# fe in row layout by a transposing transfer, out stores issued from ScalarE, and the last chunk's u in one step

## The chip, the cores and the metric

One core of one Trainium2 chip. The time is device time in microseconds (us) of one launch; the number to predict is the median over runs. TensorE is called PE, VectorE DVE, ScalarE ACT, GpSimd POOL, SyncE SP.

## What is computed

The forward pass and all gradients of a small speech encoder with a joint network (bfloat16, B=2, T=16000, D=V=256, U=8):

```python
h  = gelu(conv3(x, w1))[:, ::2]            # [2, 8000, 256]
f  = gelu(conv3(h, w2))[:, ::2]            # [2, 4000, 256]
fe = f @ w_f ;  ge = g @ w_g               # [2, 4000, 256], [2, 8, 256]
j  = tanh(fe[:, :, None, :] + ge[:, None, :, :])
out = j @ w_o                              # [2, 4000, 8, 256]
out, vjp = jax.vjp(forward, x, w1, w2, g, w_f, w_g, w_o)
return (out, *vjp(grad_out))
```

## The kernel before

The 8000 positions of `f` are cut into 17 chunks: one of 2x128, fifteen of 4x128 (`CW` = 512) and a last one of 1x64 (`LAST` = 16). Three stages work on different chunks at once: `stage_j(k)` (tanh, `out`, and what flows back to fe), `stage_a(k+1)` (convolutions, gelu, fe) and `stage_de(k-1)` (all other gradients). PE does the matmuls; ACT and DVE share the element work; SP issues nearly all transfers.

The order of instructions on each engine isn't the order of the source. `Flow.op` records every operation with a place (`F.now` or `at`, in positions: 512 of them are one full chunk), a modelled cost and what it depends on. `Flow.issue` then fills the engines one instruction at a time by modelled start time, then by place. Numbers such as 0.55 of `dt`, `late`, `land` (the time assumed between a transfer's end and its use) or `lag` (an extra wait in the model only) thus only move an operation in its engine's queue. Each engine works through its queue in that fixed order, and an instruction whose input isn't there holds up all behind it.

What the change touches, for a chunk g:

- `FE` (L593 on) holds fe with the 256 channels on partitions, as [128, 2, 512]; two evacuations write it. `stage_j` reads it for tanh into `JT` (L670), with `ge` as the bias.
- From chunk 2 on (`NTR` = 2), `fe_rows` also makes `FER`, fe with positions on partitions: 8 PE transposes into one PSUM tile (L616) and one copy (L324 or L329). For each pair of u, DVE then adds `GEB` to `FER` (L694) and ACT takes tanh in place (L699); the result `JR` is the weight operand of the matmuls into `GWO`, the gradient of w_o, which stays in PSUM for the whole run. `JR` and `OUT` each have 3 buffers. Chunks 0 and 1 make `JR` by PE transposes of `JT` (L688).
- A chunk's `stage_j` goes in 4 pairs of u. Each pair loads `GO` (grad_out), makes `GOT` from it by a transposing transfer, and stores `OUT`. All of these are issued by SP (L339 the transposing transfers, L341 the others). In the last chunk the same instructions have 64 positions instead of 128 or 512.
- The gradients of a chunk need rows too: `HR`, `GNR` and `GHR` are transposing transfers from SP, by `tile_rows`.
- The last gradients end with `last_w1`, `last_gx_stores` and small stores. At the start, ACT issues the loads of w1, w_f and w_g, and POOL that of w_o.

Of the kernel before, what the change touches and what calls it, by code (L numbers as in the profile page):

```python
# [35 lines left out]
class Flow:  # L36
# [70 lines left out]
    def issue(self):  # L107
# [14 lines left out]
        while left:  # L122
# [40 lines left out]
            if o.xfer:  # L163
                kind, work, land = o.xfer
                if e == "SP":
                    work, gap = self.ring(dma_kind, kind, work, dma_free)
                    begin = max(dma_free + gap, s + 1300.0)
                    dma_free, dma_kind = begin + work, kind
                    T[e] = max(T[e], dma_free - self.BACKLOG[kind])
                    o.done = dma_free + land  # L170
                else:
                    o.done = T[e] + work + land
            else:
                o.done = T[e] + self.TAIL[e]
# [14 lines left out]
def c_pe(ns):  # L189
    return sum(max(n / 2.4 + 2.5, 25.0) for n in ns)  # L190
# [20 lines left out]
def kernel(  # L211
# [254 lines left out]
    def conv_gelu(g_, jobs, rd, h_buf, pre, ho, gname, gcls, gshape, gsave, news):  # L466
# [39 lines left out]
        late = F.now + CW * (0.8 if g_ == 1 else 0.25)  # L506
# [34 lines left out]
    def stage_a(g_, t0, dt):  # L541
# [25 lines left out]
        F.now = t0 + 0.05 * dt  # L567
# [3 lines left out]
        F.now = t0 + 0.12 * dt  # L571
# [3 lines left out]
        F.now = t0 + 0.3 * dt  # L575
# [15 lines left out]
        F.now = t0 + 0.48 * dt  # L591
        FE = S["FE"] = buf("fe", [P, KT, CW], BF16, "FE")
        for mt in range(KT):  # L593
            ps = psum()

            def mms(e, mt=mt, ps=ps):
                for kt in range(KT):
                    mm(ps[:, :c.W], WF[:, kt, mt * P:(mt + 1) * P], HT[:, oF:oF + nb, kt, :n_], kt == 0, kt == KT - 1)
            op("PE", c_pe([c.W] * KT), mms, r=ftk + [WF], w=[ps], new=[ps] + ([FE] if mt == 0 else []))
            evac(lambda mt=mt: FE[:, mt, :c.W], lambda ps=ps: ps[:, :c.W], c.W, r=[ps], w=[(FE, mt)])  # L600
        F.now = t0 + 0.55 * dt
        if g_ >= NTR:
            fe_rows(g_)
        F.now = t0 + 0.75 * dt
        tile_rows(g_, "HR", "hr", HT, 3 * nb + 1, shape=[P, 3 * NB + 1, D], land=4500.0)

    def fe_rows(g_):
        c, S = chunks[g_], st[g_]
        nb, n_, FE = c.nb, c.np, S["FE"]
        FER = S["FER"] = buf("fer", [P, NB, D], BF16, "FER")  # L610
        ps = psum(BF16)

        def trs(e, ps=ps):
            for a in range(nb):
                for kt in range(KT):
                    nc.tensor.transpose(out=ps[:n_, (a * KT + kt) * P:(a * KT + kt + 1) * P],  # L616
                                        in_=FE[:, kt, a * n_:(a + 1) * n_], identity=ident[:])
        op("PE", c_pe([P] * (nb * KT)), trs, r=[FE, ident], w=[ps], new=[ps, FER])
        evac(lambda: FER[:n_, 0:nb].rearrange("p a d -> p (a d)"), lambda ps=ps: ps[:n_, 0:nb * D], nb * D,
             r=[ps], w=[FER], f=0.5)  # L620

    n_gwo = sum(c.nb for c in chunks) * U * KT
# [29 lines left out]
    def stage_j(g_, t0, dt):  # L654
# [4 lines left out]
        def cut(ap, lo, hi):  # L659
            return ap.rearrange("p (a n) -> p a n", a=nb)[:, :, lo:hi] if c.mid else ap  # L660

        def pair(up):
# [4 lines left out]
            for j in range(2):  # L667
                for mt in range(KT):
                    for k_, (lo, hi, b) in enumerate(parts_of(c)):
                        op("ACT", c_act((hi - lo) * nb, ptr=True), lambda e, j=j, mt=mt, lo=lo, hi=hi, b=b: nc.scalar.activation(  # L670
                            out=cut(JT[:, j, mt, :W], lo, hi), in_=cut(S["FE"][:, mt, :W], lo, hi), func=ACT.Tanh,
                            bias=GE[:, b, mt, 2 * up + j:2 * up + j + 1], scale=1.0),
                           r=[(S["FE"], mt), (GE, b)], w=[(JT, (j, mt, k_))],
                           new=[JT] if j == 0 and mt == 0 and k_ == 0 else [], at=tu - q * (1.0 - (2 * j + mt) / 4))
            npart = len(parts_of(c))
            for h in range(max(nb // 2, 1)):
                na = min(nb, 2)
                JR = buf("jr", [P, 2, 2, D], BF16, "JR")
                th = tu + q * (h / 2 - 0.5)
# [30 lines left out]
                gwo_ops.append(op("PE", c_pe([V] * (4 * na)), gwo, r=[JR, GO], w=[], at=tu + q * (h / 2 + 0.3)))  # L710
            OUT = buf("out", [P, NB, 2, V], BF16, "OUT_SB")
            for step in range(4):
# [12 lines left out]
                if d2 == 0:  # L725
                    JSQ = buf("jsq", [P, KT, CW], BF16, "JSQ")

                    def jsq(e, j=j, JSQ=JSQ):
# [5 lines left out]
                       r=[(JT, (j, mt, k_)) for mt in range(KT) for k_ in range(npart)], w=[JSQ], new=[JSQ], at=F.now - q / 4)  # L734
# [22 lines left out]
                if step < nb:  # L757
# [8 lines left out]
                    op("PE", c_pe([V] * 4), out_mm, r=[JT, WO, (OUT, "b")], w=[ps], new=[ps] + ([OUT] if a == 0 else []))  # L766
# [4 lines left out]
            dma("SP", lambda dst_=dst_: dst_, lambda OUT=OUT: OUT[:n_, 0:nb].rearrange("p a u v -> p a (u v)"), r=[OUT], w=[],  # L771
                bytes_=W * 1024)
# [5 lines left out]

    def pe_rows(g_, name, cls, SRC, lo, nblk, m):
        R = buf(cls, [P, 2 * NB + (cls == "ghr"), D], BF16, name)  # L780
# [8 lines left out]
        op("PE", c_pe([P] * (nblk * KT)), trs, r=[SRC, ident], w=[ps], new=[ps, R])  # L789
# [3 lines left out]
    def grad_rows(g_, name, cls, SRC, nblk, m):  # L793
        if chunks[g_].last:
            return pe_rows(g_, name, cls, SRC, 1, nblk, m)
# [42 lines left out]
    def stage_de(g_, t0, dt):  # L838
# [15 lines left out]
        F.now = t0 + dt * 0.05  # L854
# [68 lines left out]
        load_xr(g_, t0 - 300.0 if c.last else t0 + dt * 0.3, [got_op[0, UP - 1]] if c.first else ())  # L923
# [139 lines left out]
    def gwg_out():  # L1063
# [10 lines left out]
    CONVS = 4  # L1074
    GEBX = 1.2
# [5 lines left out]
       r=[(warm, 0)], w=[(warm, 1)])  # L1081
# [17 lines left out]
    wload("ACT", WG, 0, lambda: WG[:], lambda: w_g.rearrange("(kt p) n -> p kt n", p=P), BIG, 7000.0)  # L1099
# [5 lines left out]
    wload("POOL", WO, 0, lambda: WO[:], lambda: w_o.rearrange("(kt p) n -> p kt n", p=P), BIG + 2, 9000.0)  # L1105
# [51 lines left out]
    for k in range(NG + 1):  # L1157
        c = chunks[min(k, LAST)]
        t0, Wk = float(c.q0 if k < NG else NQ), float(c.W) if k < NG else 300.0
        if k < NG:  # L1160
            if k in (NTR, CB, CB + 1):
                load_geb(c, lambda up, t0=t0, Wk=Wk, k=k: t0 + Wk * (up / UP - (GEBX if k == NTR else 0.5)))
            for up in range(UP):
                load_go(k, up, t0 + Wk * (up // 2 * 2 / UP - 0.6), [got_op[0, up - 2]] if k == 0 and up > 1 else ())
                load_got(k, up, t0 + Wk * (up / UP - 0.6))
        if 0 < k < LAST:
            load_xc(k + 1, t0 - Wk * 0.3)
        if k < NG:
            stage_j(k, t0, Wk)
# [49 lines left out]
```

## Time and profile before

| | |
|---|---|
| median of 3 runs | 782.3 us (781.51 to 782.38) |
| profiled execution, its own time | 781.06 us |
| its span | 779.0 us, 2.06 us less than its own time |
| granted PE clock | 0.999 |
| busy: PE, DVE, ACT, POOL | 767.7, 718.2, 710.5, 84.0 us |
| transfers | 183.82 MB, 236 GB/s in the mean |
| out stores of 512 KB, issue to landing | 60 of them, 5.5 us median |

Times are microseconds from the span's start, and ns where said. A row of the grouped view has line, engine, operation, output and inputs, tile shapes, count; then busy time and the mean ns of one. In the timeline each row is a start, a length, an engine and an operation with its count; an engine name with q (ACTq, SPq) is the issuing of a transfer or a wait in that engine's queue. Matmuls overlap, so what one costs is read from one row's start to the next row's start, not from its length.

### The profile page before, as it was taken

The numbers are of one execution on the slowest core, as the hardware profiler recorded it, in microseconds if no ns is written. First come the engines' busy times: TensorE is split into PE (matmuls) and PEld (weight loads), VectorE is DVE, ScalarE is ACT, GpSimd is POOL, SyncE is SP. The second block draws the span as 40 slices with busy tenths as digits, with TensorE's granted clock in tenths as the row PEclk, the third lists the DMA queues.
The fourth block names the chain that finished last, engine by engine and source line by source line (L and its number), as shares of the span: only waits on it lengthen the run. The fifth ranks groups of instructions, "written<-read, shape, count | busy, mean of one in ns | idle before, by whom it ended". The sixth has DMA issues, their size and how long they took to land.

```text
span 779.0 us, 15414 instructions
## 1 busy us (share of the span) xinstructions
PE 767.7 (99%) x5641; PEld 533.0 (68%) x5641; DVE 718.2 (92%) x1511; ACT 710.5 (91%) x1145; POOL 84.0 (11%) x223
## 2 busy tenths in 40 slices
PE   8999999999999999999999999999999999999997
PEld 6765767576676766767577675766767667677765
DVE  4989999998999999999999999989999899999874
ACT  5989999999999999999999999899999999999752
POOL 2001010101102010020110202001020010201000
PEclk9999999999999999999999999999999999999999
DMA  9999999999999999999999999999999999989783
GB/s 182 228 250 230 230 232 265 250 228 273 205 252 241 240 293 223 280 236 238 257 252 283 204 249 252 236 283 212 272 238 223 254 223 291 191 225 244 187 177 109
DMA packets 393624, 183.82 MB, mean 236 GB/s; under 512 B 318145, under 2 KB 386668, under 8 KB 391628
## 3 DMA queue, kind: packets, MB, share of 16 engines
q1 hardware_dynamic: 391226, 181.64, 102.5%
q10 hardware_dynamic: 2178, 1.05, 0.5%
q8 instruction: 44, 0.72, 0.4%
q0 software_dynamic: 144, 0.15, 0.2%
q14 instruction: 32, 0.26, 0.1%
HBM read 52.99 MB, written 50.35 MB: 133 GB/s over the span
## 4 chain that ended last, share of the span: by engine, by line
PE 89%; ACT 6%; DVE 3%; DMA 2%; issue 1%; ACTq 0%
PE ps L315 74%; PE GWO L315 14%; ACT JT L670 2%; DMA WG<-in_w_g_dram 1%; PE psb L616 1%; ACT JSQ L730 1%; ACT HT L499 1%; ACT g_sq L497 1%; DMA W<-in_w_dram 0%; DVE NGZ L739 0%; ACT JR L699 0%; ACT OUT_SB L324 0%; DVE g_s L501 0%; DVE ZS L754 0%; ACT g_s L509 0%
## 5 line engine op out<-in xcount | busy, mean ns | idle before, releaser
L670 ACT ACTIVATE JT<-FE,GE 128x512 bf16<-128x512 bf16 (+4 forms) x288 | 178.9, 683 | 0.0
L739 DVE SCALAR_TENSOR_TENSOR NGZ<-JSQ,ps 128x512 f32<-128x512 bf16 (+3 forms) x252 | 150.8, 607 | 2.1 <-PE ps L315 1.9
L315 PE MATMUL ps<-WO,JT 128*128 128x256 bf16 (+1 forms) x1008 | 150.5, 273 | 0.3 <-DVE NGZ L739 0.2
L315 PE MATMUL ps<-GOT,WOT 128*128 128x512 bf16 (+2 forms) x544 | 149.9, 362 | 0.3 <-DVE g_s L501 0.3
L730 ACT ACTIVATE JSQ<-JT 128x1024 bf16<-128x1024 bf16 (+2 forms) x129 | 131.0, 1015 | 11.1 <-DVE NGZ L739 8.3
L315 PEld LDWEIGHTS <-JT 128*128 128x128 bf16 (+1 forms) x1008 | 98.3, 98 | 58.3 <-issue 0.4
L324 ACT CAST OUT_SB<-ps 128x512 bf16<-128x512 f32 (+1 forms) x205 | 121.7, 605 | 14.8 <-PE ps L315 14.3
L699 ACT ACTIVATE JR<-JR 128x1024 bf16<-128x1024 bf16 (+1 forms) x116 | 123.5, 1066 | 9.6 <-DVE JR L694 9.6
L315 PE MATMUL GWO<-GO_R,JR 128*128 128x256 bf16 (+1 forms) x1008 | 130.8, 273 | 0.6 <-DVE JR L329 0.6
L754 DVE TENSOR_TENSOR ZS<-ZS,NGZ 128x1024 f32<-128x1024 f32 (+2 forms) x102 | 115.3, 1130 | 0.7
L315 PEld LDWEIGHTS <-JR 128*128 128x128 bf16 (+1 forms) x1008 | 98.2, 98 | 15.8 <-DVE JR L329 0.9
L315 PEld LDWEIGHTS <-W 128*128 128x128 bf16 x636 | 60.0, 98 | 59.8 <-issue 0.7
L315 PE MATMUL ps<-W1T,GH 128*128 128x256 bf16 (+2 forms) x506 | 94.6, 325 | 1.3 <-ACT FE L324 1.2
L315 PE MATMUL ps<-XC,W 128*128 128x512 bf16 (+2 forms) x432 | 86.5, 351 | 0.1
L315 PE MATMUL ps<-GHR,XR 128*128 128x256 bf16 (+1 forms) x736 | 83.3, 273 | 0.0
L315 PEld LDWEIGHTS <-XR 128*128 128x128 bf16 (+1 forms) x756 | 73.7, 98 | 8.6
L694 DVE TENSOR_TENSOR JR<-FER,GEB 128x1024 bf16<-128x1024 bf16 (+1 forms) x116 | 78.0, 673 | 0.0
L315 PEld LDWEIGHTS <-WOT 128*128 128x128 bf16 x544 | 51.0, 98 | 29.6 <-issue 1.9
L819 DVE TENSOR_TENSOR ACC<-ACC,ps 128x512 f32<-128x512 f32 x87 | 57.4, 679 | 14.4 <-PE ps L315 14.3
L315 PEld LDWEIGHTS <-GH 128*128 128x128 bf16 (+1 forms) x506 | 49.4, 98 | 26.3 <-issue 1.9
L326 ACT ACTIVATE GX_SB<-ps 128x512 bf16<-128x512 f32 (+1 forms) x89 | 52.0, 608 | 13.8 <-PE ps L315 13.5
L497 ACT ACTIVATE g_sq<-ps 128x512 bf16<-128x512 f32 (+2 forms) x102 | 57.6, 565 | 2.8 <-PE ps L315 2.8
(131 smaller groups left out, 984.2 us busy)
## 6 DMA issues: line engine op xcount, KB each, us to landing
GO_R<-in_grad_out_dram SPq DMA_DIRECT2D x60, 512.0 KB, 5.2
out_dram<-OUT_SB SPq DMA_DIRECT2D x60, 512.0 KB, 5.5
XR<-in_x_dram SPq DMA_DIRECT2D x15, 1088.0 KB, 8.6
out_dram<-GX_SB SPq DMA_DIRECT2D x30, 512.0 KB, 3.3
GOT<-GO_R SPq DMA_TRANSPOSE x68, 5.3
GO_R<-in_grad_out_dram SPq DMA_DIRECT2D x4, 256.0 KB, 4.1
out_dram<-OUT_SB SPq DMA_DIRECT2D x4, 256.0 KB, 2.6
out_dram<-STAGE SPq DMA_DIRECT2D x6, 128.0 KB, 1.8
```

Of the source, the lines that this page charges most:

```text
L315: nc.tensor.matmul(ps_ap, lhsT=lhsT, rhs=rhs, start=start, stop=stop)
L324: nc.scalar.copy(out=dst(), in_=src())
L326: nc.scalar.activation(out=dst(), in_=src(), func=ACT.Copy, scale=scale)
L497: op("ACT", c_act(W, True), lambda e, mt=mt, ps=ps: nc.scalar.activation(out=sq[:, 0:nb, mt, :n_], in_=blk(ps, c), func=ACT.Square, scale= ...
L499: op("ACT", c_act(W, True), lambda e, mt=mt, ps=ps: nc.scalar.activation(out=h_buf[:, ho:ho + nb, mt, :n_], in_=blk(ps, c), func=ACT.Gelu_ ...
L670: op("ACT", c_act((hi - lo) * nb, ptr=True), lambda e, j=j, mt=mt, lo=lo, hi=hi, b=b: nc.scalar.activation(out=cut(JT[:, j, mt, :W], lo, h ...
L694: op("DVE", c_dve(na * 2 * D, 0.5), lambda e, h=h, na=na, JR=JR: nc.vector.tensor_tensor(out=JR[:n_, 0:na], in0=S["FER"][:n_, 2 * h:2 * h ...
L699: op("ACT", c_act(na * 2 * D), lambda e, na=na, JR=JR: nc.scalar.activation(out=JR[:n_, 0:na], in_=JR[:n_, 0:na], func=ACT.Tanh), r=[JR], ...
L730: nc.scalar.activation(out=JSQ[:, :, :W], in_=JT[:, j, :, :W], func=ACT.Square)
L739: nc.vector.scalar_tensor_tensor(out=cut(Z[:, d2, :W], lo, hi), in0=cut(JSQ[:, d2, :W], lo, hi), scalar=1.0, in1=cut(ps[:, :W], lo, hi), o ...
L754: nc.vector.tensor_tensor(out=o_, in0=i0, in1=i1, op=ALU.add)
L819: op("DVE", c_dve(512), lambda e: nc.vector.tensor_tensor(out=acc_ap().rearrange("p k d -> p (k d)"), in0=acc_ap().rearrange("p k d -> p ( ...
```

## The change

- `FE` becomes [128, 4, 2, 128], the layout that `tile_rows` takes. For chunks 2 to 15 `fe_rows` is one transposing transfer of 256 KB on SP, instead of 8 PE transposes and a copy. The last chunk has no `FER` any more.
- The `OUT` stores of chunks 0 to 15 are issued from ACT's queue, placed in the model 2.5 us after their data is there (`lag`).
- `stage_j_last` replaces `stage_j` for chunk 16: its 64 positions of 8 u are one tile of 512 columns. Two loads, one transposing transfer, 8 transposes of `JT` for `JR`, 4 matmuls of 512 columns (before 32 of 64), 8 out and 8 `GWO` matmuls with 128 positions (before 16 and 16 with 64), two stores.
- Places and model terms: longer landing times, a least PE cost of 45 ns instead of 25, the `JR` work 0.41 of a pair's time later, the `GWO` matmuls 0.04 earlier, `HR` from 0.75 to 0.43 of a chunk, the next chunk's `XC` load earlier, and others. w_o is loaded from ACT's queue instead of POOL's, and the first activation comes after those loads.

```diff
-    return sum(max(n / 2.4 + 2.5, 25.0) for n in ns)
+    return sum(max(n / 2.4 + 2.5, 45.0) for n in ns)
...
-        F.now = t0 + 0.48 * dt
-        FE = S["FE"] = buf("fe", [P, KT, CW], BF16, "FE")
+        F.now = t0 + 0.46 * dt
+        FE = S["FE"] = buf("fe", [P, NB, KT, P], BF16, "FE")
...
-        F.now = t0 + 0.55 * dt
-        if g_ >= NTR:
+        F.now = t0 + 0.63 * dt
+        if NTR <= g_ < LAST:
             fe_rows(g_)
-        F.now = t0 + 0.75 * dt
+        F.now = t0 + 0.43 * dt
         tile_rows(g_, "HR", "hr", HT, 3 * nb + 1, shape=[P, 3 * NB + 1, D], land=4500.0)

     def fe_rows(g_):
         c, S = chunks[g_], st[g_]
         nb, n_, FE = c.nb, c.np, S["FE"]
+        if not c.last:
+            return tile_rows(g_, "FER", "fer", FE, nb, shape=[P, NB, D], at=F.now - 400.0, land=7000.0)
...
-                th = tu + q * (h / 2 - 0.5)
+                th = tu + q * (h / 2 - 0.09)
...
-                gwo_ops.append(op("PE", ..., gwo, ..., at=tu + q * (h / 2 + 0.3)))
+                gwo_ops.append(op("PE", ..., gwo, ..., at=tu + q * (h / 2 + 0.26) + DEFER.get((g_, up), 0.0)))
...
-            dma("SP", lambda dst_=dst_: dst_, lambda OUT=OUT: ..., r=[OUT], w=[],
-                bytes_=W * 1024)
+            dma("SP" if c.last else "ACT", lambda dst_=dst_: dst_, lambda OUT=OUT: ..., r=[OUT], w=[],
+                bytes_=W * 1024, lag=0.0 if c.last else 2500.0)
...
+    def stage_j_last(t0):
...
+                op("ACT", ..., out=JT[:, 0, mt, u * n_:(u + 1) * n_], in_=S["FE"][:, 0, mt, :n_], func=ACT.Tanh, ...
+                   at=t0 - 64.0)
...
+        op("PE", c_pe([P] * (UP * KT)), trs, r=[JT, ident], w=[tr], new=[tr, JR])
+        evac(lambda: JR[:].rearrange("p a d -> p (a d)"), lambda: tr[:], UP * D, r=[tr], w=[JR], f=0.5)
...
+    DEFER = {(LAST - 1, 3): 100.0, (LAST - 1, 2): 130.0}
...
-    wload("POOL", WO, 0, lambda: WO[:], ..., BIG + 2, 9000.0)
+    wload("ACT", WO, 0, lambda: WO[:], ..., BIG, 7000.0)
...
-                load_go(k, up, t0 + Wk * (up // 2 * 2 / UP - 0.6), ...)
-                load_got(k, up, t0 + Wk * (up / UP - 0.6))
+                load_go(k, up, t0 + Wk * (up // 2 * 2 / UP - 0.66), ...)
+                load_got(k, up, t0 + Wk * (up / UP - 0.51))
...
-            load_xc(k + 1, t0 - Wk * 0.3)
+            load_xc(k + 1, t0 - Wk * 0.58)
...
-            stage_j(k, t0, Wk)
+            stage_j(k, t0, Wk) if k < LAST else stage_j_last(t0)
```

136 lines of the change are left out of this document (112 added, 24 removed).

## The prediction

> **What bounds the kernel now.** I read the page first: the shares of the engines, the DMA slices, and the chain that ended last.
>
> ```profile
> span 779.0 us, 15414 instructions
> PE 767.7 (99%) x5641; PEld 533.0 (68%) x5641; DVE 718.2 (92%) x1511; ACT 710.5 (91%) x1145; POOL 84.0 (11%) x223
> DMA  9999999999999999999999999999999999989783
> GB/s 182 228 250 230 230 232 265 250 228 273 205 252 241 240 293 223 280 236 238 257 252 283 204 249 252 236 283 212 272 238 223 254 223 291 191 225 244 187 177 109
> PE 89%; ACT 6%; DVE 3%; DMA 2%; issue 1%; ACTq 0%
> ```
>
> PE is idle for 11.3 us of 779.0, and it carries 89% of the chain. But three others are close behind: DVE 92%, ACT 91%, and some transfer is in flight nearly always. Since a busy PE may still be a waiting one, I then asked for two middle chunks and for the end by windows (columns: length, PE, PEld, DVE, ACT, POOL busy with counts, PE clock, DMA share, GB/s), and for PE's waits.
>
> ```profile
> 266.88:314.27 47.39, 47.39 (x339) 32.49 (x337) 44.94 (x88) 44.90 (x70) 6.01 (x14) 1.00 1.09 257
> 314.27:361.67 47.40, 47.40 (x339) 32.51 (x337) 45.07 (x88) 45.02 (x70) 5.74 (x13) 1.00 1.09 256
> ...
> 0.00:20.00 20.00, 17.29 (x158) 13.63 (x159) 9.06 (x33) 11.59 (x28) 5.76 (x20) 1.00 0.93 183
> 20.00:45.00 25.00, 22.73 (x215) 18.14 (x214) 23.64 (x58) 23.43 (x45) 1.22 (x6) 1.00 1.09 233
> ...
> 770.00:775.00 5.00, 4.57 (x36) 2.94 (x34) 4.22 (x7) 1.63 (x5) 0.00 (x0) 1.00 0.42 116
> 775.00:779.00 4.00, 0.00 (x0) 0.00 (x0) 0.04 (x1) 0.26 (x1) 0.00 (x0) 0.89 0.44 117
> ...
> PE psb L616 <- ACT FE L324: 0.2, 1, 0.2
> ```
>
> Two chunks take the same 47.4 us, PE has no gap in them at full clock, and over the whole run PE's wait for fe is 0.2 us, once. So a full chunk is a fixed list of matmuls back to back, and each matmul that leaves it shortens it, as long as DVE and ACT (95% here) and the transfers can follow. The idle PE time is at the start (5.0 us in the first 45) and at the end (4.4 us after the last matmul).
>
> **The transposes of fe.** How much goes per chunk is read from starts, since the lengths overlap (start, length, what, count):
>
> ```profile
> 304.50 0.59 PE L315 MATMUL ps<-GOT,WOT 128*128 128x512 bf16 x2
> 304.93 0.60 PE L315 MATMUL ps<-WO,JT 128*128 128x256 bf16 x4
> 305.37 1.46 PE L315 MATMUL ps<-W1T,GH 128*128 128x512 bf16 x8
> 306.67 0.66 PE L616 MATMUL psb<-ident,FE 128*128 128x128 bf16 x8
> 307.16 0.59 PE L315 MATMUL ps<-GOT,WOT 128*128 128x512 bf16 x2
> ...
> L616 PE MATMUL psb<-ident,FE 128*128 128x128 bf16 x112 | 9.0, 220 | 0.2 <-ACT FE L324 0.2
> L324 ACT COPY FER<-psb 128x1024 bf16<-128x1024 bf16 x14 | 14.3, 1022 | 0.0
> ```
>
> Eight of them hold PE for 307.16 - 306.67 = 0.49 us, 61 ns each. There are 112, so 14 chunks lose 14 x 0.49 = 6.9 us of PE that nothing covers. ACT also loses 14 copies; one holds it for 0.89 us (start 308.76 to the next start at 309.65, rows below).
>
> Here a rule speaks against the change. The Trainium skill, VectorE: DVE Perf Modes, "The three transpose paths" and "Rules for kernel authors", gives a 128x128 bf16 transpose 390 ns on TensorE against 1309 ns by a transposing DMA, and advises TensorE where PSUM will do. With its 390 ns, as an estimate, this term would be 43.7 us; this trace's stream of eight disagrees, at 61 ns each, and the trace decides.
>
> **What the transfer costs instead.** It goes into SP's queue, of 256 KB. No row has one of that size; the nearest are its neighbours, from issue to landing, and the longest issue of one that could stand ahead of it:
>
> ```profile
> HR<-HT SPq DMA_TRANSPOSE x17, 6.5
> GNR<-GN SPq DMA_TRANSPOSE x16, 4.9
> out_dram<-OUT_SB SPq DMA_DIRECT2D x60, 512.0 KB, 5.5
> ...
> 291.75 5.29 SPq L339 DMA_TRANSPOSE XC<-in_x_dram  x1
> ...
> 305.64 1.07 ACT L324 CAST FE<-ps 128x512 bf16<-128x512 f32 x2
> 306.58 1.08 ACT L699 ACTIVATE JR<-JR 128x1024 bf16<-128x1024 bf16 x1
> 313.33 0.68 DVE L694 TENSOR_TENSOR JR<-FER,GEB 128x1024 bf16<-128x1024 bf16 x1
> ```
>
> By the code `GNR` is 512 KB and `HR` 832 KB; they take 4.9 and 6.5. So between 4.9 us (nothing ahead) and 5.3 + 6.5 = 11.8 us. fe is there at 306.7, and the first add that could use it, even if it were the next chunk's, is at 313.33: 6.6 us. The change puts the adds 0.41 of a pair later, and a pair is 47.4 / 4 = 11.85 us: 4.9 us more, 11.5 together. That covers all but the worst end, so I cost the wait at nothing. If the cover fails, DVE stands at the add, everything behind it in DVE's queue (gradient products, evacuations) stands too, and PE follows through full PSUM tiles. The late add has a price of its own: add, tanh and `GWO` now have 0.35 of a pair, 4.1 us, where they had 0.8, 9.5 us. Third rival.
>
> In bytes the transfer is 0.26 MB on 47.4 us x 257 GB/s = 12.2 MB per chunk, 2.2%. The slices show up to 293 and 291 GB/s over 19.5 us, 14% above the mean of a middle chunk. I take the 2.2% as carried.
>
> **The stores from ACT.** SP is rid of 60 issues, which stood between the transposing ones, and ACT gets 60, some 4 per chunk. What one costs ACT no row shows directly. These bound it:
>
> ```profile
> 308.76 1.02 ACT L324 COPY FER<-psb 128x1024 bf16<-128x1024 bf16 x1
> 309.65 0.61 ACT L324 CAST OUT_SB<-ps 128x512 bf16<-128x512 f32 x1
> ...
> 1.24 1.28 ACT L1080 ACT_TABLE_LOAD   x1 [1.24 <-PEq L1203]
> 1.30 0.94 ACTq L341 DMA_DIRECT2D W<-in_w_dram  x2
> 2.27 0.49 ACTq L341 DMA_DIRECT2D WF<-in_w_f_dram  x1
> 4.19 0.37 ACTq L341 DMA_DIRECT2D WG<-in_w_g_dram  x1
> ```
>
> An issue takes 0.37 to 0.49 us of the queue, and two of them ran while the engine itself was in its table load. So one costs between 0 (hidden behind the activation before it) and 0.47 us; I take 0.1, nearer the first, because nearly all activations of a chunk are longer than an issue. Per chunk ACT changes by 4 x 0.1 - 0.89 = -0.5 us, with ends -0.9 and +1.0. A store waits for the last evacuation of its `OUT` tile, and tanh, squares and PSUM evacuations are queued behind it; the 2.5 us of `lag` is what hides that. The stores move the same bytes on either queue, so I count no gain in the transfers. The Trainium skill says as much (DMA: Bandwidth & Descriptors, "Issuing engines are not separate DMA queues"): all queues run on the same 16 DMA engines, and only issuing time is saved.
>
> **The last chunk.** Its matmuls of 64 positions run in a PE that has no gap until 774.57:
>
> ```profile
> 744.61 0.22 PE L315 MATMUL ps<-GOT,WOT 128*128 128x64 bf16 x2
> 744.76 0.62 PE L315 MATMUL ps<-WO,JT 128*64 128x256 bf16 x4
> 745.32 0.23 PE L315 MATMUL ps<-GOT,WOT 128*128 128x64 bf16 x2
> 745.48 0.61 PE L315 MATMUL GWO<-GO_R,JR 64*128 64x256 bf16 x4
> 746.02 0.29 PE L315 MATMUL ps<-GOT,WOT 128*128 128x64 bf16 x4
> ...
> L315 PE MATMUL ps<-GOT,WOT 128*128 128x64 bf16 x32 | 3.0, 195 | 0.0
> L315 PE MATMUL ps<-WO,JT 128*64 128x256 bf16 x16 | 2.5, 279 | 0.0
> L315 PE MATMUL GWO<-GO_R,JR 64*128 64x256 bf16 x16 | 2.4, 272 | 0.0
> ```
>
> By starts, four out matmuls take 0.56, four `GWO` 0.54, a pair of the 64-column ones 0.15: 4 x 0.56 + 4 x 0.54 + 16 x 0.15 = 6.8 us. After: 16 full matmuls of 256 columns at 0.44 / 4 (304.93 to 305.37) = 1.76, four of 512 at 0.43 / 2 = 0.86, eight transposes 0.49, together 3.1; two transposes of this chunk's fe go too, 0.1. Net -3.8 us of PE. It counts in full only if other work fills the places where these pieces stood between the dependent steps of chunk 15's gradients. The change holds back out and `GWO` work of chunk 15 (`DEFER`) for that. I take -3.2, with ends 0 and -3.8.
>
> **Start and the rest.** w_o joins ACT's queue as its sixth load, and the first activation comes after it. PE's 5.0 us of gaps there can shrink or grow; 0, with ends -3.0 (more than half of them closed) and +1.5. For places that fit less well than the gapless ones of now I add 1.0 us, 0.07 per chunk.
>
> **Sum.** -6.9 - 3.2 + 0 + 1.0 = -9.1 us against the profiled execution's 781.06 (span 779.0 and 2.06 around it): 772.0. That execution is 1.24 below the median of the runs, 782.3; in terms of the median the forecast is 773.2. All good ends together (-6.9 - 3.8 - 3.0) give 782.3 - 13.7 = 768.6. About 0.2%, 1.6 us, is what a measurement of this kernel can tell from no change.
>
> **Rivals.**
>
> *ACT and DVE become the bound.* If an issue costs ACT the full 0.47 us, ACT needs 44.9 + 1.0 = 45.9 of a 46.9 us chunk, 98%, in an order with DVE at 96%. PE's saving would come back as waits for tiles, and the chunks stay at 47.4. Left is the end: 782.3 - 3.2 = 779.1. For it: the 95% now. Against: the issues beside the table load, and the copy that goes. Chance 0.14.
>
> *The DMA engines are the bound.* Then a chunk grows by the bytes added: 0.262 MB / 257 GB/s = 1.02 us, and PE's saving is void: 782.3 + 14 x 1.02 - 3.2 = 793.4, slower. It decides where the room in a chunk is under 1.02 - 0.49 = 0.53 us. For it: the nines of the DMA slices, a share over 1, SP's issue of 5.29 us. Against: the slices of 293 and 291, with PE just as full. The Trainium skill's rule on issuing engines, cited above, is on this rival's side. Chance 0.10.
>
> *Add, tanh, `GWO` just in time.* With 4.1 us instead of 9.5, in two nearly full in-order queues, each of the 8 `GWO` groups of a chunk can wait; a late fe transfer shows at the same place. At 0.15 us for each of 14 x 8 = 112 groups it is +16.8: 773.2 + 16.8 = 790.0, slower. It decides from 9.1 / 112 = 0.08 us per group. Against: add and tanh together need 0.68 + 1.08 = 1.76 us. Chance 0.13.
>
> **How the numbers follow.** Forecast 0.63, with its own range 769 to 777. Faster by over 0.2%: 0.63, and 0.11 of the first rival, 0.74. Same: 0.04, the rest of the first and the edge of the third. Slower: 0.22, the second, most of the third. The range from 768 to 787 leaves out the second rival, the worse half of the third and little below: under 0.2.
>
> **What would show it.** L616's 112 matmuls gone; a middle chunk of 46.9 us without PE gaps; ACT busy below 710 us; out stores on ACT's queue, with no ACT wait before them; after the last 64-position tile no new PE gap; fe's transfer landing within 11 us. Wrong if a chunk stays at 47.4 with PE waiting for ACT or DVE (first), transfers land later and PE or DVE names them (second), or PE's gaps stand before `GWO` (third).

## The result, and the profile after

| | before | changed |
|---|---|---|
| median, beside each other on the chip | 782.1 us (780.32 to 783.68, 20 runs) | 777.92 us (773.52 to 782.22, 20 runs) |
| profiled execution, its own time | 781.06 us | 776.53 us |
| its span | 779.0 us | 774.4 us |

The ratio is 0.9946, 95% interval 0.9928 to 0.9963: faster by 0.54%, 4.2 us, where 9.1 were forecast. The changed kernel also spreads more, over 8.7 us where before spreads over 3.4. Executions far slower than the others of their kernel are in no ratio, and the profile of one of them, e1's (1332.68 us, at a granted clock of 0.556), is not read. First the page after: its span, its engines, the granted clock in the 40 slices, and the two big transfer queues (SP's and ACT's; packets, MB, share of 16 engines).

```profile
span 774.4 us, 14954 instructions
PE 759.7 (98%) x5491; PEld 524.0 (68%) x5491; DVE 717.5 (93%) x1483; ACT 695.9 (90%) x1110; POOL 74.7 (10%) x222
...
PEclk9999999899999999999999999999999999999999
...
q1 hardware_dynamic: 373594, 152.80, 90.8%
q10 hardware_dynamic: 35218, 33.69, 14.6%
```

PE has 150 matmuls and 8.0 us of busy time less, ACT is down by 14.6 us to 695.9, and the stores are on a queue of their own (33.69 MB). But the eighth slice of PE's clock is an 8, and PE is at 98% where it was at 99%. The windows show where (length, then busy time of PE, PEld, DVE, ACT, POOL with counts, clock, DMA share, GB/s). First before, then after:

```profile
20.00:160.00 140.00, 136.09 (x1019) 94.72 (x1018) 134.75 (x291) 134.17 (x219) 14.00 (x42) 1.00 1.11 241
260.00:400.00 140.00, 139.92 (x989) 95.84 (x988) 132.68 (x272) 134.66 (x218) 16.28 (x38) 1.00 1.09 252
```

```profile
20.00:160.00 140.00, 131.04 (x937) 87.11 (x936) 126.70 (x272) 126.00 (x204) 13.40 (x42) 0.98 1.11 237
260.00:400.00 140.00, 139.97 (x979) 95.55 (x978) 134.55 (x276) 133.22 (x214) 12.22 (x37) 1.00 1.10 255
...
259.59:306.49 46.90, 46.90 (x331) 32.10 (x328) 44.56 (x88) 44.14 (x68) 5.45 (x13) 1.00 1.10 254
...
132.00:134.60 2.60, 0.04 (x1) 0.00 (x0) 2.59 (x5) 2.60 (x5) 0.00 (x0) 1.00 0.77 173
134.60:141.40 6.80, 2.87 (x7) 1.04 (x8) 0.69 (x2) 1.86 (x3) 0.19 (x1) 0.50 1.16 278
```

A middle chunk is 46.90 us without a gap, as forecast. What is missing was lost between 20 and 160 us, where PE is idle for 9.0 us (3.9 before). Most of it is one stall, from 132.0 to 138.5 us, and the clock is at half for 6.8 us, from inside that stall (134.6) until 141.4. PE's timeline there, and two rows of PE's waits:

```profile
131.44 0.60 PE L318 MATMUL ps<-WO,JT 128*128 128x256 bf16 x4
138.53 1.04 PE L318 MATMUL ps<-GOT,WOT 128*128 128x512 bf16 x2 [6.49 <-DMA GOT<-GO_R]
```

```profile
PE ps L318 <- DMA GOT<-GO_R: 6.7, 2, 6.5
...
PE GWO L318 <- ACT JR L704: 0.5, 2, 0.3
```

And SP's queue ahead of it, after and then before (start, length of the issue):

```profile
96.46 8.47 SPq L342 DMA_TRANSPOSE GNR<-GN  x1
105.02 4.77 SPq L342 DMA_TRANSPOSE GOT<-GO_R  x2
109.85 5.16 SPq L342 DMA_TRANSPOSE GHR<-GH  x1
115.12 0.56 SPq L344 DMA_DIRECT2D GO_R<-in_grad_out_dram  x1
115.72 7.16 SPq L342 DMA_TRANSPOSE XC<-in_x_dram  x1
123.43 1.25 SPq L342 DMA_TRANSPOSE FER<-FE  x1
124.78 0.56 SPq L344 DMA_DIRECT2D GO_R<-in_grad_out_dram  x1
125.43 6.29 SPq L342 DMA_TRANSPOSE HR<-HT  x1
131.81 4.64 SPq L342 DMA_TRANSPOSE GOT<-GO_R  x1
```

```profile
113.28 10.37 SPq L339 DMA_TRANSPOSE XC<-in_x_dram  x1
123.75 2.30 SPq L339 DMA_TRANSPOSE GOT<-GO_R  x1
126.16 0.57 SPq L341 DMA_DIRECT2D out_dram<-GX_SB  x1
...
131.68 6.15 SPq L339 DMA_TRANSPOSE HR<-HT  x1
```

SP issues without a pause: each row starts where the one above it ends. Summed over all rows of 20 to 140 us, SP is issuing 94% of the time before and 96% after. The `GOT` that PE waits for (the first of chunk 3) went out at 123.75 before, ahead of `HR`; now `FER` and `HR` are ahead of it and it goes out at 131.81.

For a ledger I cut each profiled execution at the first fe matmul of each chunk (`ps<-HT,WF`), 17 marks. The rows with the first and the last start, before and after:

```profile
L315 PE MATMUL ps<-HT,WF x68: 193/379/379, 17.6 to 721.2; 128*128 128x512 bf16 x60, 128*128 128x256 bf16 x4, 128*128 128x64 bf16 x4
```

```profile
L318 PE MATMUL ps<-HT,WF x68: 193/379/390, 15.1 to 720.3; 128*128 128x512 bf16 x60, 128*128 128x256 bf16 x4, 128*128 128x64 bf16 x4
```

| us | before | changed | difference |
|---|---|---|---|
| start to the first mark | 17.59 | 15.11 | -2.5 |
| first to sixth mark (the first stretch) | 191.14 | 197.57 | +6.4 |
| sixth to sixteenth mark (the middle) | 475.17 | 470.34 | -4.8 |
| sixteenth mark to the end of the span | 95.06 | 91.41 | -3.7 |

The sum is -4.5 us, the difference of the two profiled executions. Three parts gained about what they should or more; the first stretch gave 6.4 back.

### The profile page after: what moved, and what is told of

It is laid out like the page before. It is cut to its first block, busy times and chain, and to the rows that moved or that the text cites. A ratio compares the mean times of both kernels' runs of the same rounds, so it can differ in the third digit from the quotient of the medians.

```text
span 774.4 us, 14954 instructions
## 1 busy us (share of the span) xinstructions
PE 759.7 (98%) x5491; PEld 524.0 (68%) x5491; DVE 717.5 (93%) x1483; ACT 695.9 (90%) x1110; POOL 74.7 (10%) x222
## 3 DMA queue, kind: packets, MB, share of 16 engines
q10 hardware_dynamic: 35218, 33.69, 14.6%
## 4 chain that ended last, share of the span: by engine, by line
PE 68%; DVE 12%; ACT 4%; issue 1%; SPq 1%; DMA 1%; DVEq 0%; ACTq 0%
PE ps L318 58%; PE GWO L318 10%; DVE NGZ L744 3%; DVE ZS L759 2%; ACT JR L704 1%; DVE ACC L915 1%; DMA GOT<-GO_R 1%; SPq L342 1%; DVE JR L699 1%; DVE g_sq L516 1%; DVE G L504 1%; DVE GH L998 1%; DVE GH L977 1%; DVE GX_SB L334 1%; ACT OUT_SB L327 1%
## 5 line engine op out<-in xcount | busy, mean ns | idle before, releaser
L675 ACT ACTIVATE JT<-FE,GE 128x512 bf16<-128x512 bf16 (+3 forms) x272 | 176.4, 689 | 2.6 <-DMA FER<-FE 2.6
L318 PE MATMUL ps<-GOT,WOT 128*128 128x512 bf16 (+1 forms) x516 | 148.5, 373 | 7.0 <-DMA GOT<-GO_R 6.7
L318 PE MATMUL ps<-WO,JT 128*128 128x256 bf16 x1000 | 147.6, 273 | 0.2 <-DVE ACC L332 0.2
L744 DVE SCALAR_TENSOR_TENSOR NGZ<-JSQ,ps 128x512 f32<-128x512 bf16 (+2 forms) x238 | 147.7, 630 | 0.1
L735 ACT ACTIVATE JSQ<-JT 128x1024 bf16<-128x1024 bf16 (+1 forms) x123 | 127.5, 1037 | 11.1 <-DVE NGZ L744 9.5
L318 PEld LDWEIGHTS <-JT 128*128 128x128 bf16 x1000 | 97.4, 98 | 56.0 <-issue 0.6
L318 PE MATMUL GWO<-GO_R,JR 128*128 128x256 bf16 x1000 | 129.7, 273 | 1.2 <-ACT JR L704 0.5
L327 ACT CAST OUT_SB<-ps 128x512 bf16<-128x512 f32 x193 | 112.6, 590 | 17.0 <-PE ps L318 16.1
L704 ACT ACTIVATE JR<-JR 128x1024 bf16<-128x1024 bf16 x112 | 117.5, 1060 | 3.2 <-DVE JR L699 3.1
L759 DVE TENSOR_TENSOR ZS<-ZS,NGZ 128x1024 f32<-128x1024 f32 (+1 forms) x96 | 113.4, 1181 | 0.5
L915 DVE TENSOR_TENSOR ACC<-ACC,ps 128x512 f32<-128x512 f32 x87 | 58.0, 677 | 11.9 <-PE ps L318 11.7
L329 ACT ACTIVATE GX_SB<-ps 128x512 bf16<-128x512 f32 (+1 forms) x94 | 53.9, 593 | 16.5 <-PE ps L318 12.3
```

Source lines behind the costliest of these rows:

```text
L318: nc.tensor.matmul(ps_ap, lhsT=lhsT, rhs=rhs, start=start, stop=stop)
L327: nc.scalar.copy(out=dst(), in_=src())
L329: nc.scalar.activation(out=dst(), in_=src(), func=ACT.Copy, scale=scale)
L704: op("ACT", c_act(na * 2 * D), lambda e, na=na, JR=JR: nc.scalar.activation(out=JR[:n_, 0:na], in_=JR[:n_, 0:na], func=ACT.Tanh), r=[JR], ...
L735: nc.scalar.activation(out=JSQ[:, :, :W], in_=JT[:, j, :, :W], func=ACT.Square)
L744: nc.vector.scalar_tensor_tensor(out=cut(Z[:, d2, :W], lo, hi), in0=cut(JSQ[:, d2, :W], lo, hi), scalar=1.0, in1=cut(ps[:, :W], lo, hi), o ...
```

## The experiments

The kernels are told apart by a second ledger, of the time that PE loses. Each matmul is counted at 1/2.4 ns per column (0.43 us for the 1024 columns of the two `GOT` matmuls in the prediction's rows) plus 1.5 ns, or 8.5 ns if it has 128 columns or fewer (so that a transpose comes to about the 61 ns shown there). What a stretch lasts beyond that is lost: gaps, half clock, and a small remainder even without either. "Early" is the loss from 65 to 210 us, "later" that from 210 to 660. Each is from one profiled execution.

| kernel | median us | ratio to before | early | later |
|---|---|---|---|---|
| before | 782.1 | 1 | 2.3 | 3.9 |
| changed | 777.9 | 0.9946 [0.9928, 0.9963] | 12.3 | 4.0 |
| e2: before + last chunk | 779.7 | 0.9968 [0.9953, 0.9982] | 2.3 | 3.7 |
| e3: before + start | 779.0 | 0.9966 [0.9953, 0.9979] | 2.2 | 3.7 |
| e4: before + fe transfer | 785.1 | 1.0037 [1.0016, 1.0058] | 3.5 | 16.1 |
| e9: before + stores from ACT | 782.7 | 1.0007 [0.9990, 1.0023] | 2.5 | 3.6 |
| e15: before + both | 784.3 | 1.0018 [0.9994, 1.0043] | 11.8 | 3.3 |
| e10: changed, stores on SP | 786.3 | 1.0065 [1.0050, 1.0079] | 3.4 | 18.9 |
| e8: changed, fe rows by PE | 778.3 | 0.9947 [0.9928, 0.9966] | 9.0 | 2.8 |
| e5: e1 again (below), one run | 780.7 | | 8.7 | 11.9 |
| e6: changed again, one run | 777.3 | | 11.7 | 4.8 |
| e7: changed, `XC` later early on | 777.8 | 0.9939 [0.9919, 0.9959] | 16.7 | 4.4 |
| e11: changed, old places early | 775.6 | 0.9930 [0.9915, 0.9945] | 8.9 | 7.7 |
| e14: changed, fe rows by PE early | 777.1 | 0.9943 [0.9920, 0.9965] | 6.5 | 6.6 |
| e12: both of these and `GO`'s old place; profile of its longest execution | 770.5 | 0.9869 [0.9849, 0.9890] | 10.0 | 4.2 |
| e13: e12 again | 772.8 | 0.9881 [0.9860, 0.9902] | 7.5 | 4.3 |
| e18: e12, old places in all chunks | 773.9 | 0.9906 [0.9886, 0.9925] | 8.2 | 4.2 |
| e16: changed, stores on SP early | 778.5 | 0.9987 [0.9959, 1.0016] | 2.6 | 12.8 |
| e17: e12, stores on SP early | 776.0 | 0.9930 [0.9909, 0.9952] | 1.6 | 9.1 |

"Early" in a kernel's name means the first five chunks. The medians come from several chips, so kernels are compared by the ratio, each against before on its own chip. Where the quotations speak of "the marker of chunk 5", the fifth mark is meant. The theories had letters: A, that one transfer (the `GOT` above) stands in a wrong place; C, that the transfers as a whole have no room in the first chunks, so that an order only chooses which of them is late; later S, that the stores from ACT do the harm there.

### One transfer put back: e1, e5, e6

```diff
-                load_got(k, up, t0 + Wk * (up / UP - 0.51))
+                load_got(k, up, t0 + Wk * (up / UP - (0.60 if k == 3 else 0.51)))
```

> The kernel after, with the GOT transfers of chunk 3 alone placed 0.60 instead of 0.51 of a chunk ahead; on SP's queue this puts the chunk's first GOT before the HR transfer instead of behind it. Theory A (one transfer late by its place in SP's queue): the PE gap of 6.5 us at 132 us and the stretch at half clock behind it are gone, about 7.9 us less than the 776.5 us of the profiled execution: 767 to 771 us, granted clock 0.998 or more in every run. Theory B (the transfers as a whole are short there): the wait goes to the next transfer, HR or a later GOT, PE keeps a gap of 4 us or more between 110 and 190 us, and the time stays at 775 to 779 us.

778.2 us, ratio 0.9953 [0.9935, 0.9970]: as the changed kernel. For a profile, e5 is the same kernel, and e6 is the changed one again.

> The same kernel as e1, for an undisturbed profile (e1's own was taken at a clock of 0.556). Theory A (only the place of one transfer was wrong): no PE gap over 0.5 us from 90 to 260 us; the time then must be lost elsewhere. Theory C (SP's queue is full through the first chunks, so that an order only chooses which transfer is late): PE gaps that sum to 3 us or more between 100 and 260 us, behind a transfer other than the first GOT of chunk 3 (HR, GNR, GHR or a later GOT).

> The kernel after, unchanged, for a second look at its gap at 132 us. If the gap follows the transfers' speed of the moment, it has another length (0 to 10 us) and the time moves with it, from 772 without a gap to 781; if it is fixed by the order it is 6.5 us again and the time 776.5.

One run each: e5 780.7 us, e6 777.3 us. e6 repeats the stall, 5.58 us at 132.42 for the same `GOT`. In e5 that wait is gone; its `GOT` waits are for later ones, 1.1 us at 181.9 the longest, and PE waits for `GNR` instead, 3.37 us at 151.25 and 2.98 at 250.08 (waits of PE):

```profile
PE ps L318 <- DMA GNR<-GN: 6.9, 3, 3.4
...
PE ps L318 <- DMA GOT<-GO_R: 1.3, 2, 1.1
```

Theory A falls. Putting one transfer right makes another late.

### The parts with little dispute: e2, e3

e2 is the kernel before with `load_last` and `stage_j_last` in place of the last chunk's `stage_j`:

```diff
-            for up in range(UP):
+            if k == LAST:
+                load_last(t0 - CW * LEAD)
+            for up in range(UP if k < LAST else 0):
...
-            stage_j(k, t0, Wk)
+            stage_j(k, t0, Wk) if k < LAST else stage_j_last(t0)
```

> The kernel before, with only the last chunk's eight u in one step (no transposes of its fe, its out stores still from SP). If PE has no gap until its last matmul and other work fills the places of the small matmuls: 3.6 us less, 778.5 us (777.5 to 779.5). If those places are left empty: 781 to 783 us, with PE gaps after 740 us.

-2.5 us by the ratio [1.4 to 3.7], between the two cases that I had expected. In its profile the part from the sixteenth mark to the end takes 92.28 us, 2.8 less than before.

e3 is the kernel before with the start of the change:

```diff
-       r=[(warm, 0)], w=[(warm, 1)])
+       r=[(warm, 0)], w=[(warm, 1)], at=BIG + 5.0)
...
+    wload("ACT", WO, 0, lambda: WO[:], lambda: w_o.rearrange("(kt p) n -> p kt n", p=P), BIG, 7000.0)
...
-    wload("POOL", WO, 0, lambda: WO[:], lambda: w_o.rearrange("(kt p) n -> p kt n", p=P), BIG + 2, 9000.0)
```

> The kernel before, with only the start changed: w_o loaded from ACT's queue, the first activation behind all of ACT's loads. If the start's gain of the kernel after (first fe matmul at 15.1 instead of 17.6 us) comes from these two edits: first fe matmul at 15 to 15.5 us, and 1.5 to 2.5 us less at the end, 780 us. If it comes from places later in the run: first fe matmul at 17 us or later and 782 us.

-2.7 us [1.6 to 3.7]; the first mark is at 15.07 instead of 17.59. Why is in ACT's and SP's queues of e3:

```profile
2.81 0.56 ACTq L341 DMA_DIRECT2D WG<-in_w_g_dram  x1
4.28 0.40 ACTq L341 DMA_DIRECT2D WO<-in_w_o_dram  x1
```

```profile
3.98 4.18 SPq L339 DMA_TRANSPOSE XC<-in_x_dram  x1
```

w_g goes out at 2.81, where it went out at 4.19 before and PE waited for it (1.6 us). SP's and ACT's transfers take turns on eight completion semaphores in this program, so the ninth must wait for an earlier one to land: before, that was w_g, held until the first load of w1 had landed at 4.17; in e3 it is SP's `XC`, which starts at 3.98 and not at 2.15, and PE doesn't wait for that.

### fe transfer and stores, two by two: e4, e9, e10, e15

e4 is the kernel before with fe's new layout and its transposing transfer; e9 has only the stores from ACT, and e15 has both (e9 and e15 with the change's model term for a transfer that ACT issues). In e4 and e15 the adds stand where they stood before, so fe's transfer has the 6.6 us of cover of the prediction there, not 11.5. e10 is the changed kernel, late adds included, with the stores back on SP.

```diff
+        if not c.last:
+            return tile_rows(g_, "FER", "fer", FE, nb, shape=[P, NB, D], at=F.now - 400.0, land=7000.0)
...
-            dma("SP", lambda dst_=dst_: dst_, ..., bytes_=W * 1024)
+            dma("SP" if c.last else "ACT", lambda dst_=dst_: dst_, ..., bytes_=W * 1024, lag=0.0 if c.last else 2500.0)
```

> The kernel before, with only fe's row layout by the transposing transfer (chunks 2 to 15; places and out stores as before). Theory A (a full chunk is bound by PE and the transfer is carried): middle chunks of 46.9 us instead of 47.35, 14 x 0.45 = 6.3 us less, 776 us, unless one transfer is late somewhere. Theory B (the DMA engines have no room): middle chunks stay at 47.4 us or grow to 48.4, 782 to 797 us.

> The kernel before, with only the out stores moved to ACT's queue. Theory C (in the first chunks SP's queue and the transfers are full; the stores' queue matters little): 781 to 783, no difference. Rival E (stores on a second queue take the DMA engines ahead of the transposing transfers, so PE waits longer in the first chunks): 784 to 788, with waits of PE for GOT, HR or GNR of more than 3 us before 170 us.

> The changed kernel with the out stores back on SP. Theory C: SP's queue gets four more issues per chunk where it is already full, so the stall of the first chunks stays or grows: 778 to 782, marker of chunk 5 at 165 us or later. Rival E: the stall shrinks, 772 to 776, marker of chunk 5 at 159 to 162 us.

> The kernel before with the fe transfer and the out stores from ACT, and neither the new places nor the new start nor the new end. The fe transfer alone gave 785.1 against 782.0, the stores alone 782.7 against 781.3; if they add: 785 to 786. Theory C (what limits is SP's queue; the stores' issues that leave it make the room which the fe transfer needs): 778 to 781, chunks of 46.9 us from 170 us on, losses only before.

The stores alone change nothing that can be measured (theory C's 781 to 783). The fe transfer with the stores on SP costs time: +2.9 us by the ratio in e4 and +5.1 in e10, where the same changed kernel with stores from ACT gains 4.2. e10 is out of both its ranges: the early loss is gone, as rival E had it, and the time is longer than theory C had it. The loss lies later: 16.1 and 18.9 us in the ledger, against 3 to 4. In e10 it is spread, with every full chunk after the fifth mark at 47.3 to 52.7 us. In e4 four chunks of 49.3 to 52.9 us hold it, and the other seven are at 46.9 to 47.4 with the stores still on SP. How it reaches PE is in the waits of e10, of PE, then of ACT, then of DVE:

```profile
PE GWO L318 <- ACT JR L704: 6.8, 10, 1.5
PE ps L318 <- DVE GN L759: 4.0, 2, 3.7
PE ps L318 <- DMA GOT<-GO_R: 2.3, 3, 1.3
```

```profile
ACT JR L704 <- DVE JR L699: 21.1, 26, 5.1
```

```profile
DVE JR L699 <- DMA GEB<-GED: 5.9, 2, 5.4
...
DVE JR L699 <- DMA FER<-FE: 5.0, 3, 2.8
```

DVE waits for the rows of fe and of ge, ACT's tanh waits for DVE, and PE's `GWO` for ACT. More bytes per second could have been moved. The middle windows of e10 and of e9:

```profile
260.00:400.00 140.00, 133.54 (x920) 89.25 (x919) 125.41 (x254) 123.32 (x197) 12.02 (x38) 1.00 1.07 254
```

```profile
260.00:400.00 140.00, 140.00 (x999) 96.46 (x997) 135.31 (x277) 134.26 (x211) 15.16 (x37) 1.00 1.04 248
```

e10 moves 254 GB/s and PE stands still for 6.5 us of 140; the changed kernel moved 255 in the same window and lost 0.03. From 260 to 660 us e10 moves 249 GB/s and the changed kernel 256. What differs is SP's queue: the sum of its issue times from 260 to 660 us is 89% of that time before, 75% in e9, 93% in e4 and in e10, 90% in the changed kernel. In that stretch the loss goes with this share: the kernels with 91% or more (e4, e5, e10, e11, e16) lose 6 to 17 us there, and of the others all but e14 (6.2) lose 3 to 5. But issue times are no fixed prices that add up. In e9 four stores of 0.6 us a chunk left SP, and 6.5 us a chunk of its issue time went with them, so the other issues became shorter too. Whether SP's time ran short, or the order in its one queue, or the engines behind it, no run tells apart.

But with both, e15 loses 11.8 us early, and its 784.3 is out of the 778 to 781 that I had expected. Its middle is as clean as it should be (46.90 us a chunk from 218 us on, but for two). Its waits of PE:

```profile
PE ps L318 <- DMA GOT<-GO_R: 4.3, 1, 4.3
PE ps L318 <- DMA GNR<-GN: 1.3, 1, 1.3
```

Fe's transfer and the stores together, without the rest, thus cost 1.4 us by the ratio [-0.5 to 3.4]. With the last chunk (-2.5) and the start (-2.7) that adds up to -3.8, and the whole change gave -4.2: by this sum, what it gained is its end and its start.

### What fills the first chunks: e7, e8, e11, e14, e12, e13

```diff
-            load_xc(k + 1, t0 - Wk * 0.58)
+            load_xc(k + 1, t0 - Wk * (0.3 if k < 4 else 0.58))
```

> The kernel after, with the XC load placed 0.3 instead of 0.58 of a chunk ahead for chunks 2 to 4, so that it no longer stands ahead of GOT and HR in the first chunks. Theory C (SP's queue is full there, and the early XC loads are what the late transfers wait behind): PE gaps from 90 to 260 us under 2 us in sum, 769 to 773 us. If the lack is in the transfers as a whole and not in what is issued too early: gaps as before, 776 to 780 us.

No gain, where theory C had 769 to 773; PE now waits for `XC` itself, 8.9 us in two waits (4.41 at 90.9 and 4.51 at 139.0).

e8 is the changed kernel with fe's rows by PE transposes in all chunks:

```diff
-        if not c.last:
+        if False:
             return tile_rows(g_, "FER", ...
```

> The kernel after, with fe's rows made by PE transposes and a copy again, all else left. Middle chunks go back to 47.35 us: +6.3 us. Theory C: SP's queue loses 14 transfers, the gap at 132 us shrinks or goes (-4 to -8 us), in sum 775 to 780 us. Theory A: the gap stays, 783 to 785 us.

778.3 us, inside theory C's 775 to 780. Chunks are back at 47.35 and 9.0 us of the early loss stay, 3.3 less than in the changed kernel. So fe's own transfers are not the whole of it: the stores from ACT and the new places lose 9.0 early without them, as the stores and fe's transfer lose 11.8 without the places (e15). And by the ratios (0.9947 against 0.9946) taking fe's transfer out of the changed kernel costs 0.1 us, give or take 2, where it was forecast to be worth 6.9.

e11 gives the first five chunks the old places for `XC`, `GOT` and `HR`; e14 makes their fe rows (chunks 2 to 4) on PE; e12 does both, and `GO`'s old places too.

```diff
-        F.now = t0 + 0.43 * dt
+        F.now = t0 + (0.75 if g_ < 5 else 0.43) * dt
...
-        if not c.last:
+        if not c.last and g_ >= 5:
...
-                load_go(k, up, t0 + Wk * (up // 2 * 2 / UP - 0.66), ...
-                load_got(k, up, t0 + Wk * (up / UP - 0.51))
+                load_go(k, up, t0 + Wk * (up // 2 * 2 / UP - (0.60 if k < 5 else 0.66)), ...
+                load_got(k, up, t0 + Wk * (up / UP - (0.60 if k < 5 else 0.51)))
...
-            load_xc(k + 1, t0 - Wk * 0.58)
+            load_xc(k + 1, t0 - Wk * (0.3 if k < 4 else 0.58))
```

> The changed kernel with the places of before for XC, GOT and HR in chunks below 5, later chunks unchanged; fe's transfer stays in all of them. Theory C: fe's transfers still have no room, the loss moves to another transfer and only part of it comes back: 775 to 778. Rival P (the places alone make the stall): marker of chunk 5 at 159 to 161 us, 770 to 773.

> The changed kernel with fe's rows by PE transposes in chunks 2 to 4 only; the places stay those of the change. With e11 (only the old places: 775.6) and e12 (both: 770.5) this completes two by two. Theory C with the queue full for both reasons: about half of the 7 us comes back, 774 to 776. If the three fe transfers are the whole loss: 770 to 772. If the places of XC, HR and GOT are: 777 to 778, as changed.

> The changed kernel with the first five chunks' transfers as before: places of XC, GO, GOT and HR of before, and fe's rows by PE transposes there; from chunk 5 on as changed. Theory C: the early chunks give no more back than before, so the start's 3 us, 0.45 us in each of some ten chunks and the end's 3 us are kept: 771 to 774. If the stores from ACT or the other places make the loss, marker of chunk 5 stays at 164 us or later and the time at 776 to 779.

> The same kernel as e12, for a second profile, since the profiled execution of e12 was the longest of its five (777.3 us, the others 769.7 to 773.7). Theory C with chance in the first chunks: 770 to 773 as a median, and a profile near it has the marker of chunk 5 at 158 to 161 us (start 3 us earlier than before, no stall), chunks of 46.9 us after it and 86 to 88 us from the last marker but one to the end. If instead the marker stays at 165 us in a run of 770 us, the gain came from later chunks and theory C's place for it is wrong.

Places alone: 0.9930, PE rows alone: 0.9943, neither clear of the changed kernel's 0.9946. Both, and `GO`'s place: 0.9869 and 0.9881. That beats both kernels, by 9 to 10 us against before, the size that was forecast for the change. But the fifth mark of e13 is at 161.79, not at 158 to 161: its stall is only smaller. Its row in the waits of PE:

```profile
PE ps L318 <- DMA GNR<-GN: 3.0, 2, 2.8
```

### Where the stores go: e16, e17, e18

By then all kernels with the stores on SP had an early loss of 2.2 to 3.5 us, and all with stores from ACT, but e9, one of 6.5 or more. So e16 and e17 put the stores of the first five chunks back on SP, in the changed kernel and in e12:

```diff
-            dma("SP" if c.last else "ACT", ...
-                bytes_=W * 1024, lag=0.0 if c.last else 2500.0)
+            dma("SP" if c.last or g_ < 5 else "ACT", ...
+                bytes_=W * 1024, lag=0.0 if c.last or g_ < 5 else 2500.0)
```

> The changed kernel with the out stores of the first five chunks on SP, as before, and from ACT after that; fe's transfer everywhere. From the profiles so far, first marker to sixth: 190.6 to 191.4 us where stores are on SP (before, e4, e10), 193 to 202 with stores from ACT and the changed places or the fe transfer; sixth to sixteenth: 470 with stores from ACT and the fe transfer, 483 to 485 with stores on SP and the fe transfer. Theory S (in the first chunks the stores from ACT hurt, later they make the room): stretches of about 191.5 and 470.5, together with start 15, end 87.5 and 6 that is 770 to 772. Theory C in its first form (fe transfers and places fill the first chunks, stores matter little there): first stretch stays at 195 to 198, 776 to 778.

> e12 (places of before and fe's rows by PE in the first chunks) with the out stores of the first five chunks on SP as well, so that all transfers of the first chunks are as before. Theory S: first stretch 191 to 192 instead of 194 to 198, sixth to sixteenth marker 470.5, 769 to 771, and less spread than e12's 769.7 to 777.3. Theory C in its first form: no difference from e12 and e13, 770.5 to 773.

Half of theory S came true: the early loss is gone, 2.6 and 1.6. But both are slower than without the edit (0.9930 against 0.9869, and 0.9987 against 0.9946, where the intervals overlap a little), and from 210 to 260 us, where the stores change over, they lose 5.1 and 5.3 us, against 0.4 in the changed kernel. Both wait for `GNR` there, 2.41 us at 248.92 in e16 and 2.47 at 246.81 in e17, with half clock behind it. e17 by windows:

```profile
246.80:249.30 2.50, 0.03 (x2) 0.02 (x2) 2.04 (x5) 2.24 (x5) 0.16 (x1) 1.00 1.11 220
249.30:250.00 0.70, 0.70 (x7) 0.63 (x8) 0.00 (x0) 0.70 (x2) 0.19 (x1) 0.96 0.73 158
250.00:253.30 3.30, 3.30 (x17) 2.38 (x16) 1.67 (x3) 0.55 (x1) 0.00 (x0) 0.50 1.24 277
```

After that e17's chunks are 46.90 to 47.6 us; e16 still has some of 48.8. The last kernel asked whether the earlier places are the debt that is paid there: e12 with the old places of `XC`, `GO`, `GOT` and `HR` in all chunks.

> e12 with the places of before for XC, GO, GOT and HR in all chunks, not in the first five alone; fe's rows by PE in chunks 2 to 4, by transfer after that, stores from ACT. In the profiles so far PE loses 5 to 8 us once, wherever the changed order of transfers sets in: at 132 us as changed, at 151 in e13, at 247 in e16 and e17, and nothing comparable before or in e9. Theory L (a full queue in which XC and HR are called a third of a chunk earlier must find that lead once, and PE pays for it): no such loss here, 766 to 769. Rival F (the fe transfers themselves need the lead): the loss stays, near chunk 5 (210 to 260 us), 771 to 774. Rival M (the old places don't fit the fe transfer, as in e4): small waits in many chunks, 774 or more.

773.9 us, and the loss is still in the first chunks (8.2 early). The four places alone are not its cause, and none of the three theories gave its place and its time together.

**What stays open.** An early loss of 4 to 14 us above that of before is paid in one wait or a few, in every kernel that has the stores on ACT from the start together with another edit of the transfers, and with the stores it moves (e16, e17). It is in none with the stores on SP, nor in e9. By itself it is not one transfer's place (e1, e7), not fe's transfer (e8), not the four places (e18). SP's share of issuing doesn't explain it: from 20 to 140 us it is 93 to 97% in every kernel, 96% in e17, which lost 1.6 early, and 94% in e13, which lost 7.5. Left are the other places and terms of the model, which decide when SP's queue runs ahead; they were not tried one by one. So it is shown which edits lose the time, and not by what mechanism.

## Why the prediction was wrong

The direction was right. 777.9 us lies inside the range of 768 to 787, though just above the forecast's own 769 to 777, and it is inside by some luck: 2.5 us came from the start, which was taken as 0. By its own steps:

- **The transposes of fe**: right as far as PE goes. Chunks are 46.90 us, 0.45 to 0.49 less, and the middle's ten chunks gave 4.8 of the -6.9.
- **What the transfer costs instead**: this step failed. I costed the wait at nothing, from the cover in one middle chunk, for all 14 chunks, and the middle alone bears that out. The first stretch should have been 3 x 0.49 = 1.5 us shorter, and was 6.4 longer: 7.9 us, more than the whole miss. By the ratios, fe's transfer and the stores, which together were to bring 6.9, cost 1.4 (e15, -0.5 to 3.4), and inside the change fe's transfer brings 0.1, give or take 2 (e8). The 11.5 us of cover were long enough for a transfer once it is issued: where a profile shows it (e4, e10, e15), fe's landed 3.2 to 6.4 us after its issue. What I left out is the time before the issue, in SP's queue, which issues 94% of 20 to 140 us already before; fe's transfer and `HR` went ahead of the `GOT` that PE then waited for. Nor was 5.29 us the longest issue that could stand ahead: an `XC` load held SP for 10.37 us at 113 us of the same profile. That the stall needs the stores on ACT as well is shown; why it does stays open.
- **The stores from ACT**: the cost to ACT was right (busy 695.9, under 710; issues beside running activations, rows below). "No gain in the transfers" holds for the stores alone (e9), and not beside the fe transfer: there the move is worth about 15 us of the middle (18.9 against 4.0), and early it costs what e16 and e17 move about. The rule of the Trainium skill that I cited (DMA: Bandwidth & Descriptors, "Issuing engines are not separate DMA queues") goes on to say that only the time to start a transfer is saved, usually small. A store's own issue is small here too, 0.6 us of the 5.5 to its landing; yet with four of them a chunk, 6.5 us of SP's issue time went (e9).
- **The last chunk**: right, -3.2 forecast; the end is 3.7 shorter with the 0.5 of that chunk's fe transposes in chunk 15. Alone it gave 2.5 (e2).
- **The start**: -2.5 to -2.7 where I took 0, inside its ends.
- **Places**: +1.0 for fifteen small misfits; none show in the middle. What the new places cost came early, in one stall: with the stores, and without fe's transfer, the early loss is 9.0 (e8).
- **The rivals**: ACT and DVE as the bound did not happen. The DMA engines as the bound named the right kind of thing (PE waits for transfers) at the wrong place: not every chunk but mostly one stall. That a transfer stood late in SP's queue is shown; that the engines had nothing to do with it is not. Add, tanh and `GWO` just in time is what e10 shows, 6.8 us of PE's waits, but not the changed kernel with its 0.5.

Of the sum, then: forecast -9.1, measured in the profiles -4.5; the first stretch is worse by 7.9 than its share, the start better by 2.5 and the places by 1.0.

## What to carry to other kernels

Before a transfer is added, look at the queue it goes into, stretch by stretch, and not only at the bytes: SP's was issuing 94% of the first chunks here, and a cover read from a middle chunk says nothing of them. A high share is a warning and not a price, since kernels with 96% there lost 1.6 us (e17) and 12.3 (the changed one). Judge a change by the fill of the pipeline as well as by a middle chunk, since the same edit can be free in the one and cost its whole gain in the other. Measure the parts of a change alone and in pairs: here the end and the start alone add up to 5.2 us, and the whole gain is 4.2. And when a stall moves to another transfer as soon as its own is mended (e1, e7), moving single transfers doesn't help.

## What the runs showed of the hardware

- A gap of PE can cost more than itself. In the gap of 6.49 us the granted clock fell to 0.50 after 2.6 us and stayed there for 6.8; behind gaps of 2.00 us (e12), 2.47 (e17), 2.72 (e14) and 2.79 (e13) it was 0.50 for 3.4. PE worked at half clock for 2.9 us behind the stall of the changed kernel, which thus costs 6.5 + 2.9 / 2 = 7.9 us of the ledger's 12.3 - 2.3 = 10.0; the rest lies in gaps of under 1 us, most of them from 70 to 110 us. The Trainium skill (TensorE: Matmul & The Clock Gate, "HAM oscillation — how this bites in real kernels") warns of idle gaps above about 3.4 us; here one of 2.0 was enough. Not always: a gap of 3.70 us in e10 (at 377.6) had none of it, nor had e18's longest, 2.50 us:

```profile
153.60:156.30 2.70, 0.20 (x2) 0.10 (x2) 2.54 (x6) 2.52 (x6) 0.46 (x2) 1.00 0.99 197
156.30:157.00 0.70, 0.70 (x8) 0.62 (x8) 0.00 (x0) 0.70 (x1) 0.19 (x1) 1.00 0.78 174
157.00:160.00 3.00, 3.00 (x30) 2.70 (x28) 2.35 (x4) 0.76 (x2) 0.00 (x0) 1.00 1.26 283
```

- Issuing a store from ACT is hidden behind an activation. In the changed kernel an issue of 0.54 us starts 0.34 us into an activation of 1.06 us, and the next one follows without delay:

```profile
233.59 1.06 ACT L704 ACTIVATE JR<-JR 128x1024 bf16<-128x1024 bf16 x1
233.93 0.54 ACTq L344 DMA_DIRECT2D out_dram<-OUT_SB  x1
234.55 1.05 ACT L735 ACTIVATE JSQ<-JT 128x1024 bf16<-128x1024 bf16 x1
```

- How long SP is held by one transposing issue is not set by its size: `XC` held it for 10.37 us at 113 us before and for 5.29 at 292, and a `GOT` of 512 KB, in chunks 1 to 15 of the changed kernel, for 1.83 to 8.66.
